# PSUM banks split 3/3/2, kernel rows by quarters, rows three blocks ahead, first loads in one queue, and dummy matmuls at the start

## The chip, the cores and the metric

The kernel runs on one core of a Trainium2 chip. The metric is the device time in microseconds of one execution. Lower is better.

## What is computed

The program computes a layer and all its gradients. The input x (2048 tokens, D = 576) is normalised, and three branches are added:

```python
xn  = layernorm(x)                                # over D
out = x + S4(xn) + FFN(xn)
# S4: y = irfft(rfft(xn) * rfft(K))[:L] + xn * Dskip, one kernel K of 2048 taps for each of 576 channels
dt  = exp(log_dt); logdA = dt * (A_re + 1j * A_im)
P   = exp(logdA[:, :, None] * l)                  # 576 x 128 x 2048
K   = einsum("dn,dnl,dn->dl", C, P, dt * B).real
# FFN: gate = xn @ W_gate; up = xn @ W_up        (576 x 4608)
#      h = gate * (gate > 0) * up; h @ W_down    (4608 x 576)
```

It returns `out` and the gradients of x, the six S4 parameter arrays, log_dt, Dskip and the three FFN weights for a given `grad_out`. Inputs and outputs are bf16.

## The kernel before

Two generators make the program, and a main loop interleaves them.

**FFN** (`Ffn.gen`). The hidden dimension is cut into 12 chunks of 384. In a chunk the tokens go by in four groups (`sg`) of four blocks of 128. `a_unit` multiplies one group by 128 columns of gate, up and down weights (L235, three PSUM tiles one after the other), and ACT and DVE make hT, dgT and duT from them (L243 to L255). `t_steps` turns these with PE (L264) for the weight gradients. `outdx` makes the output and the gradient of xn for one block of 128 tokens (L291: four PSUM groups of 3, 3, 6 and 6 matmuls of 288 columns), each group copied to `osx` (L67), and adds the tile to `acc_dram` by a DMA on POOL's queue (L304). After the last group of a chunk come the weight gradients: `dw_down` in four blocks (L329, 48 matmuls each), `dw_gu` in four (L345) and `dw_left` (L363). Each of these nine blocks needs one `rows` tile, which `rows` loads (L316) from the pool `ffn_d` of three buffers; block i asks for the blocks up to i + 2, and the first three of a chunk are asked for in its third group.

**S4** (`S4.gen`). The convolution is a transform in two steps with matrices of 128 and 16 points. It works in two halves of 288 channels. `p1` transforms xn and the gradient (`fwd1` L590, `mix` L604 and L605), multiplies them, and goes back to the kernel's gradient dk, which is kept whole in SBUF and stored with one DMA (L701). `p2` makes the kernel K and the sums for the parameter gradients, four channels at a time: DVE forms Y (L821 to L824), PE multiplies and turns it (`turn`, L849 and L859), `sums` multiplies it by dk (L873) and DVE reduces it (L877, L878); K goes to `k_dram` in groups of 32 channels (L852). `p3` loads K in one DMA (L710), transforms it and forms the S4 parts of the output and the gradient, stored to `C_ydu` (L742). The order is p1 of half 0; p2 of half 0 with p1 of half 1; p2 of half 1 with p3 of half 0; p3 of half 1.

**Order of the work.** Each step yields an estimate of its PE time, and S4 steps follow FFN steps in the ratio `PACE` = 0.9. S4 starts once all four layernorm groups are written. In the last chunk, `Final` adds the S4 parts to the FFN's, and all that is left of S4 is written before it. A DMA that waits on a queue (SP carries nearly all, POOL those of `acc_dram` and `xs_dram`, ACT those of `wf`) holds what comes after it on this queue. The order of instructions on an engine in the profile is not always that of the source: the load of x for the second group, for one, stands on SP ahead of the stores of the first.

**PSUM.** Eight banks are cut into three pools: `psum_mm` (FFN, 4 tiles), `psum_s4` (S4, 2 tiles) and `psum_t` (transposes for FFN and layernorm, 2 tiles). `Balance.copy` (L55 to L69) sends each copy out of PSUM to DVE or ACT by a running sum of estimated work, to which `bal.add` adds.

**The start.** `ln_group` loads x, makes mean and variance on DVE (L126, L127), normalises (L143, L144), turns the result (L147, L148) and stores it three times (`xT_dram`, `xn_dram`, and `xs_dram` on POOL's queue, L152). For the first group the down weights and the first block of `gT` are loaded in between, and `first` (L202) does the matmuls that need no layernorm while x is worked on.

Of the kernel before, what the change touches and what calls it, by code (L numbers as in the profile page):

```python
# [14 lines left out]
P = 128  # L15
# [6 lines left out]
ST = 16  # L22
# [12 lines left out]
PACE = 0.9  # L35
W1, W2, W3 = 60.0, 400.0, 58.0
# [41 lines left out]
def make_consts(g):  # L78
    nc, consts = g.nc, g.consts
    g.ident_bf = consts.tile([P, P], BF16, name="ident_bf")  # L80
    make_identity(nc, g.ident_bf[:])
    g.ident_f = consts.tile([P, P], F32, name="ident_f")
    make_identity(nc, g.ident_f[:])
    g.hpcol = consts.tile([P, 1], F32, name="hpcol")
    nc.vector.memset(g.hpcol[:], math.pi / 2)
    warm = consts.tile([P, 1], F32, name="warm")
    nc.scalar.activation(warm[:], g.hpcol[:], ACT.Sqrt)
    g.rinv = consts.tile([P, ST], F32, name="rinv")
    g.dsk_acc = consts.tile([P, NK, NSG], F32, name="dsk_acc")
# [15 lines left out]
def ln_group(g, pools, sg, loads=None, grad=None):  # L105

    nc, bal = g.nc, g.bal
    sb, small = pools
    t0 = sg * JS
    x4 = sb.tile([P, JS, D], BF16, name="x4")  # L110
    if sg == 0:
        for j in range(0, JS, 2):
            nc.sync.dma_start(x4[:, j:j + 2], g.x_v[:, j:j + 2, :])
        loads[0]()
    else:
        nc.sync.dma_start(x4[:], g.x_v[:, t0:t0 + JS, :])
    gT = g.xtp.tile([P, NK, JS * P], BF16, name="gT")
    nc.sync.dma_start(gT[:], g.gT_in[sg])
    if sg == 0:
        loads[1]()  # L120
        grad(gT)
    mv = small.tile([P, JS, nc.vector.BN_AGGR_DIM], F32, name="mv")
    for j in range(JS):
        stats = small.tile([P, 2, nc.vector.BN_STATS_DIM], F32, name="stats")
        for s in range(2):
            nc.vector.bn_stats(out=stats[:, s, :], in_=x4[:, j, s * DH:(s + 1) * DH])  # L126
        nc.vector.bn_aggr(out=mv[:, j, :], in_=stats[:])  # L127
    mvb = small.tile([P, JS, 2], BF16, name="mvb")
    nc.vector.tensor_copy(mvb[:], mv[:])
    mvf = small.tile([P, JS, 2], F32, name="mvf")  # L130
    nc.vector.tensor_copy(mvf[:], mvb[:])
    veb = small.tile([P, JS], BF16, name="veb")
    nc.vector.tensor_scalar(veb[:], mvf[:, :, 1], 1e-5, None, op0=ALU.add)
    sdb = small.tile([P, JS], BF16, name="sdb")
    nc.scalar.activation(sdb[:], veb[:], ACT.Sqrt)
    sdf = small.tile([P, JS], F32, name="sdf")
    nc.vector.tensor_copy(sdf[:], sdb[:])
    nc.vector.reciprocal(g.rinv[:, t0:t0 + JS], sdf[:])
    xn4 = sb.tile([P, JS, DP], BF16, name="xn4")
    nc.gpsimd.memset(xn4[:, :, D:DP], 0.0)  # L140
    xT = g.xtp.tile([P, NK, JS * P], BF16, name="xT")
    for j in range(JS):
        nc.vector.tensor_scalar(x4[:, j, :], x4[:, j, :], mvf[:, j, 0:1], None, op0=ALU.subtract)  # L143
        nc.vector.tensor_scalar(xn4[:, j, 0:D], x4[:, j, :], g.rinv[:, t0 + j:t0 + j + 1], None, op0=ALU.mult)  # L144
        pt = g.psum_t.tile([P, 8, P], BF16, name="pt")
        for k in range(NK):
            nc.tensor.transpose(out=pt[:, k, :], in_=xn4[:, j, k * P:(k + 1) * P], identity=g.ident_bf[:])  # L147
        nc.vector.tensor_copy(xT[:, :, j * P:(j + 1) * P], pt[:, 0:NK, :])  # L148
    nc.sync.dma_start(g.xT_dram[sg], xT[:])
    nc.sync.dma_start(g.xn_dram[:, t0:t0 + JS, :], xn4[:, :, 0:D])  # L150
    for k, d0, dsz in dchunks():
        nc.gpsimd.dma_start(g.xs_dram[k][:, t0:t0 + JS, :], xn4[:, :, d0:d0 + dsz])  # L152
    bal.add(d=7.5, a=0.3)
    return xT, gT

class Ffn:
    def __init__(self, g, ctx, Wd_in, Wf_in, dWg, dWu, dWd):
# [15 lines left out]
        self.dp = pool("ffn_d", 3)  # L173
# [10 lines left out]
    def load_wf(self, c):  # L184

        self.g.nc.scalar.dma_start(self.wf[:], self.Wf_in[c])

    def load_x(self, c, sg):
        g, nc = self.g, self.g.nc
        xT = g.xtp.tile([P, NK, JS * P], BF16, name="xT")  # L190
        nc.sync.dma_start(xT[:], g.xT_dram[sg])
        gT = g.xtp.tile([P, NK, JS * P], BF16, name="gT")
        nc.sync.dma_start(gT[:], g.gT_in[sg])
        self.X[(c, sg)] = (xT, gT)
# [112 lines left out]
    def rows(self, c, i):  # L307

        g, nc = self.g, self.g.nc
        for n in range(i, min(i + 3, 4 + NK)):  # L310
# [59 lines left out]
    def gen(self, ln, final):  # L370

        lu = FTC - 1
        for c in range(NFC):
            if c == 0:
                self.X[(0, 0)] = ln(0, (lambda: self.load_wd(0, (2,)), lambda: self.load_wd(0, (0, 1))), self.first)
                self.load_wf(0)
                for ft in range(FTC):
                    yield from self.a_unit(0, 0, ft)
                self.X[(0, 1)] = ln(1)
# [23 lines left out]
            for sg in range(1, NSG):  # L403
                todo = list(range(JS))
                for ft in range(FTC):
# [6 lines left out]
                    if c == 0 and ft == 0 and sg < 3:  # L412
                        self.X[(0, sg + 1)] = ln(sg + 1)
# [45 lines left out]
class S4:  # L459
    def __init__(self, g, par_in, log_dt, outs, Dskip):  # L460
# [8 lines left out]
        self.dk_dram = two("dk_dram", [P, DH // SC, ST, SC])  # L469
        self.k_dram = two("k_dram", [P, DH // SC, ST, SC])  # L470
# [108 lines left out]
    def fwd1(self, hf, ns, load, ap, n):  # L579
# [3 lines left out]
        for n2 in range(ST):  # L583
            if n2 % 2 == 0:
                S1, sig = Sx.get(n2 // 2), sigs.get(n2 // 2)
            A = ap.tile([P, ns, 2, DH], BF16, name=f"fA{ns}")
# [55 lines left out]
    def p1(self, hf, n, gap):  # L642
# [3 lines left out]
        with ExitStack() as c:  # L646
# [7 lines left out]
            yield from self.fwd1(hf, 2, load, ap, n)  # L654
# [29 lines left out]
        with ExitStack() as c:  # L684
            bp = self.pool(c, f"p1_c{hf}", n + 1, "right")
            dk = self.pool(c, f"p1_d{hf}", 1, "right").tile([P, DH // SC, ST, SC], BF16, name="dk")
# [6 lines left out]
            for n2 in range(ST):  # L693
# [5 lines left out]
                g.bal.copy(dk[:, :, n2, :], self.back2(S3[:, n2 % 2], Ct, 0).rearrange("p (g d) -> p g d", d=SC), DH)  # L699
                yield 0.5  # L700
            nc.sync.dma_start(self.dk_dram[hf][:], dk[:])  # L701

    def p3(self, hf, n, gap):

        g, nc, bal = self.g, self.g.nc, self.g.bal
        with ExitStack() as c:
            kp = self.pool(c, f"p3_k{hf}", 1, "right")
            ap = self.pool(c, f"p3_a{hf}", n, "right")
            kk = kp.tile([P, DH // SC, ST, SC], BF16, name="kk")
            nc.sync.dma_start(kk[:], self.k_dram[hf][:])  # L710
            yield gap
            yield from self.fwd1(hf, 1, lambda m: (lambda i, n2: kk[:, :, n2, :]), ap, n)
        with ExitStack() as c:
# [13 lines left out]
            for h in range(ST + 1):  # L727
# [9 lines left out]
                if old is not None:  # L737
                    Ct = fp.tile([P, 2, 2, DH], BF16, name="fC2")
                    for i in range(2):
                        yield from self.back1(Ct, i, old[i])  # L740
                        yield 0.7
                    nc.sync.dma_start(self.rows(self.C[2][hf], h - 1), Ct[:])  # L742
# [9 lines left out]
    def p2(self, hf, pools, pw):  # L752
# [12 lines left out]
        def load_dk(i):  # L765
            dkr = dkp.tile([P, ST, SC], BF16, name="dkr")
            nc.sync.dma_start(dkr[:], self.dk_dram[hf][:, i])
            return dkr
        exq, dkq = Ahead(load_ex, DH // SX, 2), Ahead(load_dk, DH // SC, 2)
        for gi in range(DH // SC):  # L770
# [7 lines left out]
            for x0 in range(0, SC, SX):  # L778
# [34 lines left out]
                for dd in range(x0, x0 + SX, DG):  # L813
# [5 lines left out]
                    U = uvp.tile([P, DG, 2, P], BF16, name="U")  # L819
                    V = uvp.tile([P, DG, 2, P], BF16, name="V")  # L820
                    v.tensor_tensor(vw(U), Ap(0), Bp(1), op=ALU.mult)  # L821
                    v.tensor_tensor(vw(V), Ap(1), Bp(0), op=ALU.mult)  # L822
                    Y = yop.tile([P, DG, 2, P], BF16, name="Y")
                    v.tensor_tensor(Y[:], U[:], V[:], op=ALU.add)  # L824
# [16 lines left out]
    def turn(self, item, ytp, turned):  # L841
# [9 lines left out]
        if dd + DG == SC:  # L851
            nc.sync.dma_start(self.k_dram[hf][:, gi], Kst[:])  # L852
# [193 lines left out]
def kernel(  # L1046
# [33 lines left out]
    g.psum_mm = pool("psum_mm", 4, space=PSUM)  # L1080
    g.psum_s4 = pool("psum_s4", 2, space=PSUM)
# [14 lines left out]
    ln_pools = [lnctx.enter_context(tc.tile_pool(name=n, bufs=4)) for n in ("ln_sb", "ln_small")]  # L1096
    done = [0]
# [83 lines left out]
```

## Time and profile before

| | us |
|---|---|
| median of 3 runs | 1874.34 |
| lowest and highest | 1871.84, 1876.11 |
| the profiled execution | 1874.97 |
| its span, first to last instruction | 1873.2 |

| engine | busy us | share of the span |
|---|---|---|
| PE (matmul) | 1759.1 | 94% |
| DVE | 1329.5 | 71% |
| ACT | 1161.1 | 62% |
| POOL | 216.9 | 12% |

The mean granted TensorE clock was 0.987, and the DMA queues moved 373.26 MB, 199 GB/s on average. A row of the page reads: line, engine, operation, output and inputs by name, shapes, count | busy time, mean ns of one | idle time of that engine just before, and what ended most of it. A row of waits reads: the waiting engine and line, what ended the wait, us in total, times, longest. A row of the timeline reads: start and length in us, engine, line, operation, count, and in brackets the idle time before it and its releaser. `ps_s_...` in the profile are the tiles of `psum_s4`, `ps_mm` those of `psum_mm`, `pt` those of `psum_t`. PE's row of a matmul includes the time in which it drains, which overlaps the next one.

### The profile page before, as it was taken

To read this page: it belongs to the slowest core of one execution; us is meant where nothing else is said; L and a number is where in the kernel's file an instruction comes from. 1 tells how busy PE (TensorE), PEld (TensorE's weight loads), DVE (VectorE), ACT (ScalarE), POOL (GpSimd) and SP (SyncE) were. 2 spreads that over 40 slices of the span, in tenths; PEclk is the share of its full clock that TensorE was granted. 3 is DMA by queue.
4 is the path that set the end of the run, shared out by engine and by line. 5 is a ranking of instruction groups with operands and counts; after the bars stand their busy time and mean duration, and the time that the engine had idled before them with its cause. 6 is when DMAs were issued, how large, how long until landed. Compare 5 with 4: busy or idle time off the path is not lost.

```text
span 1873.2 us, 41646 instructions
## 1 busy us (share of the span) xinstructions
PE 1759.1 (94%) x16246; PEld 1220.9 (65%) x16389; DVE 1329.5 (71%) x3052; ACT 1161.1 (62%) x2606; POOL 216.9 (12%) x264
## 2 busy tenths in 40 slices
PE   6988998999999999999899999999999998999989
PEld 3665556667667666766666766766766765676656
DVE  7574693678687787686597789787887863743872
ACT  3875775687487477477367658658747735742442
POOL 3200012022012002102101101102201100110000
PEclk9999999999999999999999999999999999999999
DMA  9698989567557566767756746855745759884763
GB/s 330 205 332 292 318 230 274 193 155 215 171 136 190 185 165 154 201 172 179 221 156 157 224 148 140 222 166 120 213 146 127 172 181 260 250 242 153 250 206 119
DMA packets 186106, 373.26 MB, mean 199 GB/s; under 512 B 19826, under 2 KB 95604, under 8 KB 183860
## 3 DMA queue, kind: packets, MB, share of 16 engines
q1 hardware_dynamic: 158900, 300.39, 48.1%
q0 software_dynamic: 25280, 54.28, 18.2%
q10 hardware_dynamic: 1728, 15.93, 2.4%
q8 instruction: 128, 2.10, 0.4%
q14 instruction: 70, 0.57, 0.1%
HBM read 233.08 MB, written 137.43 MB: 198 GB/s over the span
## 4 chain that ended last, share of the span: by engine, by line
PE 48%; DVE 16%; DMA 10%; ACT 8%; issue 6%; POOL 1%; SPq 1%; ACTq 0%; DVEq 0%; POOLq 0%
PE ps_mm L235 12%; PE ps_mm L291 10%; PE ps_mm L345 10%; PE ps_mm L329 4%; DMA acc_dram<-osx 3%; DMA rows<-in_gq_dram 3%; PE pt L264 2%; DVE pr L877 2%; DVE Sm L878 1%; DMA f_xg<-in_grad_out_dram 1%; PE ps_mm L363 1%; DVE Y L824 1%; DVE U L821 1%; ACT osx L67 1%; DVE V L822 1%
## 5 line engine op out<-in xcount | busy, mean ns | idle before, releaser
L67 ACT CAST osx<-ps_mm 128x288 bf16<-128x288 f32 x679 | 259.1, 426 | 73.2 <-PE ps_mm L291 56.9
L304 POOL DMA_DIRECT2D acc_dram<-osx x160 | 139.4, 875 | 1112.2 <-ACT osx L67 770.8
L291 PE MATMUL ps_mm<-wf,dgT 128*128 128x288 bf16 x1152 | 209.3, 286 | 2.2 <-ACT dhb L67 0.9
L291 PE MATMUL ps_mm<-wf,duT 128*128 128x288 bf16 x1152 | 208.2, 287 | 0.0
L345 PEld LDWEIGHTS <-rows 128*128 128x128 bf16 x1536 | 146.3, 98 | 91.0 <-issue 2.5
L291 PE MATMUL ps_mm<-wf,hT 128*128 128x288 bf16 x1152 | 186.7, 288 | 1.2 <-DVE hT L247 0.8
L235 PE MATMUL ps_mm<-xT,wd_97 128*128 128x512 bf16 x712 | 182.2, 380 | 0.5
L235 PE MATMUL ps_mm<-gT,wd_98 128*128 128x512 bf16 x697 | 180.9, 384 | 0.3
L329 PE MATMUL ps_mm<-rows,hN 128*128 128x144 bf16 x2304 | 163.7, 231 | 16.8 <-DMA rows<-in_gq_dram 15.2
L235 PE MATMUL ps_mm<-xT,wd_96 128*128 128x512 bf16 x593 | 168.6, 380 | 7.0 <-DVE xT L148 0.6
L329 PEld LDWEIGHTS <-hN 128*128 128x128 bf16 x2304 | 152.8, 100 | 20.0 <-DMA rows<-in_gq_dram 9.3
L245 DVE SCALAR_TENSOR_TENSOR upm<-rg,ps_mm 128x512 bf16<-128x512 bf16 x144 | 98.4, 683 | 92.4 <-PE ps_mm L235 66.5
L345 PE MATMUL ps_mm<-dgN,rows 128*128 128x384 bf16 x768 | 140.2, 328 | 0.0
L345 PE MATMUL ps_mm<-duN,rows 128*128 128x384 bf16 x768 | 138.4, 326 | 0.0
L67 ACT CAST obw<-ps_mm 128x384 bf16<-128x384 f32 x106 | 50.5, 477 | 140.0 <-PE ps_mm L345 101.6
L291 PEld LDWEIGHTS <-duT 128*128 128x128 bf16 x1152 | 112.5, 98 | 32.7 <-issue 4.1
L291 PEld LDWEIGHTS <-dgT 128*128 128x128 bf16 x1152 | 109.5, 98 | 31.7 <-issue 5.7
L291 PEld LDWEIGHTS <-hT 128*128 128x128 bf16 x1152 | 107.8, 98 | 29.1 <-DVE hT L247 3.0
L824 DVE TENSOR_TENSOR Y<-U,V 128x1024 bf16<-128x1024 bf16 x144 | 99.0, 687 | 38.2 <-PE ps_s_4388 L859 20.9
L243 ACT ACTIVATE rg<-ps_mm 128x512 bf16<-128x512 f32 x144 | 87.0, 604 | 61.8 <-PE ps_mm L235 57.5
L67 ACT CAST dhb<-ps_mm 128x512 bf16<-128x512 f32 x141 | 83.8, 594 | 63.8 <-PE ps_mm L235 61.4
L878 DVE TENSOR_REDUCE Sm<-pr 128x8 f32<-128x256 f32 x288 | 119.9, 416 | 4.6
(2893 smaller groups left out, 3567.5 us busy)
## 6 DMA issues: line engine op xcount, KB each, us to landing
acc_dram<-osx POOLq DMA_DIRECT2D x176, 288.0 KB, 4.8
gT<-in_gT_dram SPq DMA_DIRECT2D x48, 640.0 KB, 5.8
xT<-xT_dram SPq DMA_DIRECT2D x44, 640.0 KB, 5.2
rows<-in_gq_dram SPq DMA_DIRECT2D x48, 576.0 KB, 4.9
wf<-in_Wf_dram ACTq DMA_DIRECT2D x12, 1296.0 KB, 8.7
ex_dram<-exs SPq DMA_DIRECT2D x18, 640.0 KB, 4.5
ex<-ex_dram SPq DMA_DIRECT2D x36, 320.0 KB, 3.5
out_dram<-obw SPq DMA_DIRECT2D x96, 96.0 KB, 2.4
```

The lines of the kernel that those rows point to most:

```text
L67: self.nc.scalar.copy(out, in_)
L235: nc.tensor.matmul(ps[:], lhsT=w[:, k, fs], rhs=rhs[:, k, :], start=(k == 0), stop=(k == NK - 1))
L243: nc.scalar.activation(rg[:], ps_g[:], ACT.Relu)
L245: nc.vector.scalar_tensor_tensor(upm[:], rg[:], 0.0, ps_u[:], op0=ALU.is_gt, op1=ALU.mult)
L264: nc.tensor.transpose(out=pt[:, j, :], in_=src[:, j * P:(j + 1) * P], identity=g.ident_bf[:])
L291: nc.tensor.matmul(ps[:, :DH], lhsT=lt, rhs=rh, start=(i == 0), stop=(i == len(mms) - 1))
L304: nc.gpsimd.dma_start(g.acc_dram[:, t, :, :], o[:], accum_op=ALU.add)
L329: nc.tensor.matmul(ps[:, ft * 144:(ft + 1) * 144], lhsT=self.hN[:, st, ft * P:(ft + 1) * P], rhs=gq[:, st, :], start=(st == 0), stop=(st = ...
L345: nc.tensor.matmul(ps[:, :Fc], lhsT=xs[:, st, 0:P], rhs=src[:, st, :], start=(st == 0), stop=(st == ST - 1))
L824: v.tensor_tensor(Y[:], U[:], V[:], op=ALU.add)
L877: nc.vector.tensor_tensor(pr[:], X[:, dx:dx + DG, r0:r0 + 2].rearrange("p d r a -> p d (r a)").unsqueeze(2).to_broadcast(sh), psg[:, 0:DG ...
L878: nc.vector.tensor_reduce(out=Sm[:, vi, s0 + dd:s0 + dd + DG, :], in_=pr[:], op=ALU.add, axis=AX.X)
```

## The change

The pools get 3, 3 and 2 banks. `ffn_d` gets a fourth buffer, and `rows` asks for blocks up to i + 3. dk is stored, and K loaded, in four pieces of four rows each, through two rotating tiles; both DRAM tensors are laid out by quarters, so that the loads of dk by 32 channels, and the stores of K, are made of runs of 256 bytes. `fwd1` takes the `gap` yield of its caller and gives it after its first loads are issued; `p1` had none there. `C_ydu` is stored in two halves. The first product of Y is written to Y itself, and U is gone.

At the start all x groups, the weights and `wf` are loaded on SP's queue in a fixed order; `wf` is no longer on ACT's for the first chunk. 60 matmuls of 128 columns on the identity, into a `psum_s4` tile that nothing uses but one small copy, precede all others. Half of the subtractions and of the xT copies of the layernorm go to ACT, and the `xs_dram` stores from POOL's queue to SP's.

```diff
+WARM = 60
...
+    ps = g.psum_s4.tile([P, 512], F32, name="ps_s4")
+    for i in range(WARM):
+        nc.tensor.matmul(ps[:, 0:P], lhsT=g.ident_bf[:], rhs=g.ident_bf[:], start=True, stop=True)
+    nc.scalar.copy(warm[:], ps[:, 0:1])
...
+def ln_load(g, sb, sg, pieces=1):
+    nc = g.nc
+    x4 = sb.tile([P, JS, D], BF16, name="x4")
+    n = JS // pieces
+    for j in range(0, JS, n):
+        nc.sync.dma_start(x4[:, j:j + n], g.x_v[:, sg * JS + j:sg * JS + j + n, :])
+    return x4
...
-        nc.vector.tensor_scalar(x4[:, j, :], x4[:, j, :], mvf[:, j, 0:1], None, op0=ALU.subtract)
+        if j % 2 == 0:
+            nc.vector.tensor_scalar(x4[:, j, :], x4[:, j, :], neg[:, j:j + 1], None, op0=ALU.add)
+        else:
+            nc.scalar.activation(x4[:, j, :], x4[:, j, :], ACT.Identity, bias=neg[:, j:j + 1])
+    for j in range(JS):
...
-        nc.vector.tensor_copy(xT[:, :, j * P:(j + 1) * P], pt[:, 0:NK, :])
+        (nc.vector.tensor_copy if j % 2 == 0 else nc.scalar.copy)(xT[:, :, j * P:(j + 1) * P], pt[:, 0:NK, :])
...
-        nc.gpsimd.dma_start(g.xs_dram[k][:, t0:t0 + JS, :], xn4[:, :, d0:d0 + dsz])
-    bal.add(d=7.5, a=0.3)
+        nc.sync.dma_start(g.xs_dram[k][:, t0:t0 + JS, :], xn4[:, :, d0:d0 + dsz])
+    bal.add(d=6.5, a=2.5)
...
-        self.dp = pool("ffn_d", 3)
+        self.dp = pool("ffn_d", 4)
...
-        for n in range(i, min(i + 3, 4 + NK)):
+        for n in range(i, min(i + 4, 4 + NK)):
...
-                self.X[(0, 0)] = ln(0, (lambda: self.load_wd(0, (2,)), lambda: self.load_wd(0, (0, 1))), self.first)
-                self.load_wf(0)
+                xs = [ln_load(g, self.ln_sb, 0, 2)]
+                self.load_wd(0, (2,))
+                gT = self.load_gT(0)
+                self.load_wd(0, (0, 1))
+                xs.append(ln_load(g, self.ln_sb, 1))
+                self.load_wf(0, g.nc.sync)
+                xs += [ln_load(g, self.ln_sb, sg) for sg in (2, 3)]
+                self.first(gT)
+                self.X[(0, 0)] = ln(0, xs[0], gT)
...
-        self.dk_dram = two("dk_dram", [P, DH // SC, ST, SC])
-        self.k_dram = two("k_dram", [P, DH // SC, ST, SC])
+        self.dk_dram = two("dk_dram", [P, 4, DH // SC, 4, SC])
+        self.k_dram = two("k_dram", [P, 4, DH // SC, 4, SC])
...
                 S1, sig = Sx.get(n2 // 2), sigs.get(n2 // 2)
+                if n2 == 0:
+                    yield gap
...
-            dk = self.pool(c, f"p1_d{hf}", 1, "right").tile([P, DH // SC, ST, SC], BF16, name="dk")
+            dp = self.pool(c, f"p1_d{hf}", 2, "right")
...
+                if n2 % 4 == 0:
+                    dk = dp.tile([P, DH // SC, 4, SC], BF16, name="dk")
...
+                if n2 % 4 == 3:
+                    nc.sync.dma_start(self.dk_dram[hf][:, n2 // 4], dk[:])
...
+            def load(m):
+                if m % 2 == 0:
+                    kks[0] = kp.tile([P, DH // SC, 4, SC], BF16, name="kk")
+                    nc.sync.dma_start(kks[0][:], self.k_dram[hf][:, m // 2])
+                kk = kks[0]
+                return lambda i, n2: kk[:, :, n2 % 4, :]
+            yield from self.fwd1(hf, 1, load, ap, n, gap)
...
-                    Ct = fp.tile([P, 2, 2, DH], BF16, name="fC2")
                     for i in range(2):
-                        yield from self.back1(Ct, i, old[i])
+                        Ct = fp.tile([P, 1, 2, DH], BF16, name="fC2")
+                        yield from self.back1(Ct, 0, old[i])
+                        nc.sync.dma_start(self.rows(self.C[2][hf], h - 1)[:, i:i + 1], Ct[:])
...
-                    v.tensor_tensor(vw(U), Ap(0), Bp(1), op=ALU.mult)
+                    v.tensor_tensor(vw(Y), Ap(0), Bp(1), op=ALU.mult)
                     v.tensor_tensor(vw(V), Ap(1), Bp(0), op=ALU.mult)
-                    v.tensor_tensor(Y[:], U[:], V[:], op=ALU.add)
+                    v.tensor_tensor(Y[:], Y[:], V[:], op=ALU.add)
...
-            nc.sync.dma_start(self.k_dram[hf][:, gi], Kst[:])
+            nc.sync.dma_start(self.k_dram[hf][:, :, gi], Kst[:].rearrange("p (q a) d -> p q a d", q=4))
...
-    g.psum_mm = pool("psum_mm", 4, space=PSUM)
-    g.psum_s4 = pool("psum_s4", 2, space=PSUM)
+    g.psum_mm = pool("psum_mm", 3, space=PSUM)
+    g.psum_s4 = pool("psum_s4", 3, space=PSUM)
```

## The prediction

> **What bounds the kernel now.** I read the busy shares and slices of the page first, then the waits of PE, then the timeline at the three places where PE's slices are below 9.
>
> ```profile
> PE 1759.1 (94%) x16246; PEld 1220.9 (65%) x16389; DVE 1329.5 (71%) x3052; ACT 1161.1 (62%) x2606; POOL 216.9 (12%) x264
> PE   6988998999999999999899999999999998999989
> PEclk9999999999999999999999999999999999999999
> ```
>
> PE is the bound: no other engine is above 71%. A matmul that stops no one costs its slot (the chain of waits has twelve L291 matmuls in 1.47 us, 0.1225 us each, although the row says 286 ns, because their ends overlap), so only what lengthens the row of slots can be won or lost. PE is idle for 1873.2 - 1759.1 = 114.1 us. The waits of PE say for what:
>
> ```profile
> PE ps_mm L329 <- DMA rows<-in_gq_dram: 15.2, 6, 5.1
> PE ps_mm L202 <- DMA gT<-in_gT_dram: 11.0, 1, 11.0
> PE ps_s_25857 L590 <- ACT fA_25837 L67: 3.1, 1, 3.1
> PE ps_s_4243 L590 <- DMA sig<-xn_dram: 3.0, 1, 3.0
> PE ps_s_17634 L859 <- DVE pr L877: 1.9, 1, 1.9
> PE ps_mm L329 <- ACT osx L67: 1.5, 2, 1.0
> ```
>
> Added up, all rows of this view: the start 11.0; rows 15.2; matmuls into ps_s4 behind ACT or DVE 37.0, in some sixty small rows; matmuls into ps_s4 behind a DMA 10.5; transposes for FFN and layernorm 16.2; matmuls into ps_mm behind ACT or DVE 6.2. The small pool of two banks waits, the large one of four hardly does. A further cost stands in no row of waits: the mean granted clock is 0.987, so about 0.013 x 1873 = 24 us of clock are lost, in stretches that follow an idle PE:
>
> ```profile
> 20.00:34.00 14.00, 10.72 (x60) 5.48 (x61) 13.75 (x46) 2.85 (x6) 3.60 (x5) 0.88 1.04 373
> 296.00:312.00 16.00, 10.76 (x85) 8.29 (x85) 0.00 (x0) 5.76 (x16) 8.34 (x8) 0.79 1.02 287
> 905.00:925.00 20.00, 15.02 (x149) 12.62 (x146) 14.71 (x33) 2.74 (x5) 2.52 (x2) 0.83 0.72 232
> ```
>
> (Columns: stretch, length, then busy time of PE, PEld, DVE, ACT, POOL, the clock, the DMA share, GB/s.)
>
> **The start.**
>
> ```profile
> 11.02 5.87 PE L202 MATMUL ps_mm<-gT,wd_98 128*128 128x512 bf16 x15 [11.02 <-DMA gT<-in_gT_dram]
> 19.17 1.24 PE L235 MATMUL ps_mm<-xT,wd_96 128*128 128x512 bf16 x5 [0.58 <-DVE xT L148]
> 29.88 1.25 PE L147 MATMUL pt<-ident_bf,xn_350 128*128 128x128 bf16 x10 [0.86 <-DVE xn_350 L144]
> 31.72 1.93 PE L235 MATMUL ps_mm<-xT,wd_96 128*128 128x512 bf16 x5
> ```
>
> wf (1.3 MB) now leaves on ACT's queue at 0.82 us and shares the DMA engines with x, wd2 and gT (1.7 MB). The change queues it behind x1. At the 311 to 361 GB/s of these microseconds, 1.7 MB land about 5 us after the first 2 us, so gT is there near 7 us, not at 11.0. The fifteen L202 matmuls take 0.427 us each, against 0.216 us for the L235 ones from 19.17 on: they run at half rate, 15 x 0.21 = 3.2 us. The sixty dummies address that. The Trainium skill (TensorE: Matmul & The Clock Gate, The HAM clock gate) says that the array starts at half clock, needs about 3.4 us of sustained work to be released, and falls back after a comparable idle time. By that rule the dummies, waiting only for the identity (1.5 us), run 32 at 107 ns and 28 at 56 ns (the page's gaps, so an estimate) and end near 6.6 us; with gT at 7 us the release holds and 3.2 us are won, with gT at 11 us it is lost again and they win nothing. The trace alone (clock 0.5 from about 30 us, after PE's waits for xn_350) says the same about falling back; I take the win. Should the clock stay at half, 60 x 107 ns ends at 8 us and delays first by 1 us. x lands about 2.5 us earlier too, so the first L235 comes at about 13.5, not 19.2. In 20 to 34 us DVE is the bound (13.75 of 14 us). Each layernorm group loses two subtractions (0.34 us each), two xT copies (0.49) and one cast (0.17) to ACT or nothing, about 1.8 of 10 us, and pays one neg (0.17). PE's full flow at 31.7 should begin near 26. Against it: ACT, at 17.1 of 20 us in 60 to 80, gets this work; SP takes over 20 xs stores (POOL 0.76 us each; SP's DMA issues take 0.33 to 0.6, so 10 us of SP time), which wait there for xn with gT of the next group behind them, needed only by a third matmul group 10 us later. I take -6 us; bounds +2 and -11.
>
> **Rows ahead.** Only the fourth block of a chunk is late: three buffers hold blocks 0 to 2 some 95 us early, while block 3 is asked for when block 0 has been used (L316 at 610.2, 908.5, 1671.1), and needs 6 to 9 us to land, against two blocks of 48 matmuls at 0.0625 us, 6 us, plus whatever S4 puts between. At 908 it is worse because SP stands at the kk load:
>
> ```profile
> 899.99 0.33 SPq L852 DMA_DIRECT2D k_dram_135<-Kst  x1
> 908.04 0.33 SPq L710 DMA_DIRECT2D kk<-k_dram_135  x1
> 908.46 0.38 SPq L316 DMA_DIRECT2D rows<-in_gq_dram  x1
> ```
>
> With four buffers block 3 is early like the others, and each later block one block earlier. The 15.2 us go, and the half clock after 142, 914 and 1680 us (1.7 + 3.4 + 1.7 us by the clock of those stretches). The copies and stores that caught up meanwhile, and the next late transfer, take some back: -17; bounds -6 and -22. SP still waits at kk for the last Kst store; behind it only later rows and dkr then stand, with a block to spare.
>
> **Quarters and gaps.** At the first hand-over SP waits until 291.9 for one 1152 KB dk store (7.4 us to landing) before dkr, and the sig loads leave at 294.4: PE waits 3.0 us at 299.1 and runs at half clock until 309 (3.4 us lost). The last quarter store is a fourth of the size, and fwd1 now yields its gap (3 us of FFN work) after the loads are issued. -4; bounds +1 and -8. The added gaps (10 and 3 us) put S4's end about 14 us later in FFN's time; S4 ends at 1665.6 and its outputs are first needed at 1723, so 57 us of cover hide it. If that cover were gone, its last steps would run alone, at most those 14 us.
>
> Costs: C_ydu in halves, 32 more stores of 0.33 us on SP; dk and kk quarters, 6 more each; together 15 us of SP time over the span, hidden while SP is not late. Each half store waits for its own evictions, with b_k and s_ug loads behind it; the waits of SP at L723 are 61.7 us now and hardly reach PE (3.7 us, once). dkr loads and Kst stores now have runs of 256 bytes, 36 x 512 = 18432 packets. No such packet is in the trace; the nearest, 512 or 576 bytes, took 31 ns each, which makes 0.57 ms over 16 engines, 36 us of DMA time in a stage of 1200 us at a share of 0.61 to 0.76. The Trainium skill's page DMA: Bandwidth & Descriptors (Specifications) says that below 512 bytes a transfer no longer runs at line rate, which speaks against this edit: twice the price, an estimate, would be 72 us, 6% of the stage, and dkr is asked for a whole group ahead. I take +3 for all this; bounds 0 and +12. Y in place of U costs DVE nothing (the same three products); it only moves the wait for a Y buffer from L824 two instructions up, with its 20.9 us (once, near 293 to 314) unchanged.
>
> **PSUM 3/3/2.** What two banks cost S4:
>
> ```profile
> 315.98 0.36 PE L873 MATMUL ps_s_4489<-dkc,YT 128*128 128x32 bf16 x8
> 316.38 0.42 DVE L877 TENSOR_TENSOR pr<-X,ps_s_4489 128x256 f32<-128x256 f32 x1 [0.28 <-PE ps_s_4489 L873]
> 316.44 0.35 PE L849 MATMUL ps_s_4520<-XC,Y 128*128 128x16 bf16 x8
> 316.83 0.21 ACT L67 CAST Kst<-ps_s_4520 128x64 bf16<-128x64 f32 x1 [0.44 <-PE ps_s_4520 L849]
> 317.09 0.61 PE L859 MATMUL ps_s_4530<-ident_bf,Y 128*128 128x128 bf16 x8
> 317.29 0.42 DVE L877 TENSOR_TENSOR pr<-X,ps_s_4489 128x256 f32<-128x256 f32 x1
> ```
>
> The sums' bank is read twice by DVE and held to 317.7; so the transposes of L859 wait for the Kst copy of the other bank and start 50 ns after it. With a third bank they need not. The 37.0 us of the view are too small, since a matmul's drawn end hides the first 0.16 us of every wait; from start to start against the slots I count about 75 us at ps_s4. Of these some 18 stay (single waits where ACT itself was held up, as at 155, 306, 1002 and 1570, and the stretch 90 to 115 where ACT is busy 22.6 of 25 us). Of the other 57 I take 60%, -34: PE arrives earlier, the evictions do not. Bounds -57 and -10.
>
> The price is at ps_mm. I set each ps_mm group's first matmul beside the end of the eviction three groups before it, from the same timeline: 98 of about 1350 groups would start before it, by 40 us in total, 25 us when a delay already suffered is not counted again. They are outdx groups (slots of 0.37 us, an eviction of 0.43 us on ACT, often behind a 0.6 us hN copy), and groups after an a_unit, which takes all three banks while the up bank waits for DVE. I take +20; bounds +2 and +40.
>
> Sum: -6 - 17 - 4 + 3 - 34 + 20 = -38 us. The profiled execution took 1874.97, of which 1.8 us lie around its span, 0.6 above the median of 1874.34: 1836.
>
> **Rivals.**
> - The stalls only change pool. PE's lead is bounded by the six banks together, and these stay six; S4's 34 come back at ps_mm. For it: ACT does 679 of 704 osx copies. Against it: 37.0 beside 6.2 us is no balanced split. Then -24: 1850.
> - Slower: three banks serve FFN as badly as two serve S4. Place: a_unit followed by outdx in 1100 to 1500, where DVE is busy about 80 of each 100 us and upm frees the up bank late. S4 pays 35 ns (view) to 72 ns (slots) for each of 1046 allocations; FFN has about 1350, so 47 to 97 us. It decides from +58 at ps_mm (43 ns each). At 75 us: 1874 + 17 = 1891.
> - More: every removed stop also keeps the clock full (half of the 24 us), and S4's waits vanish nearly whole: -60, 1814.
> - The dummies find gT late, or the rows are late by another transfer: the start and rows give 10, not 23: 1849, inside the first rival's place.
>
> **How the numbers follow.** The forecast 0.47, stalls change pool (with late gT) 0.27, more 0.13, slower 0.10, nothing measurable 0.03. A measurement of this kernel can tell about 0.2%, 3.7 us, from no change. Faster: 0.47 + 0.13 + 0.26 = 0.86; same 0.04; slower 0.10. The range runs from 1804, past the "more" case, to 1868, past the changed pool; outside it lie the slower case and nothing measurable.
>
> **What would show it.** Right: L202 near 7.5 us at 0.216 us a matmul; no PE row L329 <- DMA rows; ps_s4 rows under 15 us; ps_mm rows behind ACT or DVE between 10 and 30; clock above 0.99. Wrong: ps_mm rows above 50 us; L235 and L291 waiting for upm and osx through 1100 to 1500; rows still late; S4 alone at the end.

## The result and the profile after

The changed kernel took 1860.6 us (median of four runs, 1856.6 to 1864.5) beside 1875.1 us for the kernel before: a ratio of 0.9926, 95% interval 0.9901 to 0.9950. That is 14 us faster; 38 were forecast. Two later sets of runs gave 0.9934 and 0.9930, so 12 to 14 us is a firm number. The profiled execution took 1864.5 us with a span of 1862.4, and its mean granted clock was 0.991 instead of 0.987.

The engines' busy time and PE's slices, from the page after:

```profile
PE 1753.3 (94%) x16449; PEld 1222.3 (66%) x16449; DVE 1327.2 (71%) x3041; ACT 1164.1 (63%) x2618; POOL 204.7 (11%) x244
PE   7989999999999999999989999999999998989889
```

PE is still the bound, with 109 us of idle time instead of 114. Its largest waits after the change (waiting engine and line, what ended the wait, us in total, times, longest):

```profile
PE ps_mm L300 <- ACT osx L68: 9.8, 21, 2.2
PE ps_mm L211 <- DMA gT<-in_gT_dram: 8.7, 1, 8.7
PE pt L273 <- DVE dgT L262: 6.5, 4, 2.6
...
PE ps_s_25937 L608 <- ACT fA_25907 L68: 4.7, 1, 4.7
...
PE ps_s_4087 L657 <- DMA bC_4031<-C_dk_191: 3.7, 1, 3.7
PE ps_s_27457 L622 <- ACT fC_27423 L70: 3.5, 1, 3.5
```

No row of PE waiting for `rows` is left. What is new is the first row, FFN's outdx (L300, L291 before) waiting for its eviction; before, it was 0.2 us. The last two rows are longer than any of their kind before, where the longest wait for bC was 1.4 us and the longest for fC 1.1. All rows of this view summed, for the kernels that this document turns on (us; a wait at ps_mm that a DMA ended is in a column of its own; the clock is that of the profiled execution):

| | ps_s behind ACT, DVE | ps_mm behind ACT, DVE | ps_mm behind a DMA | mean clock |
|---|---|---|---|---|
| before | 37.0 | 6.2 | 26.2 | 0.987 |
| before with 3/3/2 alone (e5) | 14.3 | 32.1 | 25.0 | 0.993 |
| changed | 36.0 | 34.7 | 8.7 | 0.991 |
| changed with 4/2/2 (e1) | 57.1 | 11.9 | 10.1 | 0.992 |
| best version (e11) | 20.1 | 31.2 | 15.0 | 0.991 |

The second and third lines hold the case. The third bank brings S4's waits in this view from 37 to 14 when it comes alone. In the whole change they are back at 36: other parts of the change put new ones in their place.

### The profile page after: what moved, and what is told of

Its sections match the earlier page's. It is cut to its first block, busy times and chain, and to the rows that moved or that the text cites. A ratio compares the mean times of both kernels' runs of the same rounds, so it can differ in the third digit from the quotient of the medians.

```text
span 1862.4 us, 42002 instructions
## 1 busy us (share of the span) xinstructions
PE 1753.3 (94%) x16449; PEld 1222.3 (66%) x16449; DVE 1327.2 (71%) x3041; ACT 1164.1 (63%) x2618; POOL 204.7 (11%) x244
## 4 chain that ended last, share of the span: by engine, by line
PE 52%; DVE 22%; DMA 12%; ACT 8%; issue 5%; SPq 1%; POOL 1%; ACTq 0%; DVEq 0%; POOLq 0%
PE ps_mm L244 13%; PE ps_mm L300 12%; PE ps_mm L354 10%; PE ps_mm L338 6%; DMA acc_dram<-osx 3%; PE pt L273 2%; DVE pr L902 2%; DVE Sm L903 2%; DVE Y L849 2%; DMA f_xg<-in_grad_out_dram 2%; DVE V L848 1%; DVE Y L847 1%; DVE upm L254 1%; DMA ex_dram<-exs 1%; PE ps_mm L372 1%
## 5 line engine op out<-in xcount | busy, mean ns | idle before, releaser
L300 PE MATMUL ps_mm<-wf,dgT 128*128 128x288 bf16 x1152 | 205.6, 287 | 16.6 <-ACT osx L68 9.8
L300 PE MATMUL ps_mm<-wf,duT 128*128 128x288 bf16 x1152 | 206.1, 287 | 0.0
L300 PE MATMUL ps_mm<-wf,hT 128*128 128x288 bf16 x1152 | 184.3, 288 | 6.0 <-DVE hT L256 3.5
L244 PE MATMUL ps_mm<-xT,wd_158 128*128 128x512 bf16 x720 | 180.1, 379 | 4.0 <-DVE osx L62 1.9
L244 PE MATMUL ps_mm<-xT,wd_159 128*128 128x512 bf16 x720 | 180.0, 379 | 0.0
L338 PE MATMUL ps_mm<-rows,hN 128*128 128x144 bf16 x2304 | 161.1, 228 | 0.0
L338 PEld LDWEIGHTS <-hN 128*128 128x128 bf16 x2304 | 150.7, 99 | 7.4 <-issue 4.1
L300 PEld LDWEIGHTS <-dgT 128*128 128x128 bf16 x1152 | 110.2, 98 | 54.0 <-issue 27.5
L354 PE MATMUL ps_mm<-dgN,rows 128*128 128x384 bf16 x768 | 136.4, 326 | 0.6 <-ACT rg L252 0.6
L300 PEld LDWEIGHTS <-duT 128*128 128x128 bf16 x1152 | 112.7, 98 | 29.1 <-issue 0.5
L300 PEld LDWEIGHTS <-hT 128*128 128x128 bf16 x1152 | 108.0, 98 | 34.3 <-DVE hT L256 5.4
L244 PEld LDWEIGHTS <-wd_160 128*128 128x128 bf16 x705 | 64.7, 98 | 67.9 <-issue 12.9
```

Source lines behind the costliest of these rows:

```text
L244: nc.tensor.matmul(ps[:], lhsT=w[:, k, fs], rhs=rhs[:, k, :], start=(k == 0), stop=(k == NK - 1))
L300: nc.tensor.matmul(ps[:, :DH], lhsT=lt, rhs=rh, start=(i == 0), stop=(i == len(mms) - 1))
L338: nc.tensor.matmul(ps[:, ft * 144:(ft + 1) * 144], lhsT=self.hN[:, st, ft * P:(ft + 1) * P], rhs=gq[:, st, :], start=(st == 0), stop=(st = ...
L354: nc.tensor.matmul(ps[:, :Fc], lhsT=xs[:, st, 0:P], rhs=src[:, st, :], start=(st == 0), stop=(st == ST - 1))
```

## The experiments

The kernel before ran beside each set of runs (1871.1 to 1873.8 us). Ratios are against it, with 95% intervals. Microseconds in the text are the differences of ratios times 1873. Within 0.2%, about 4 us, two single ratios can't be told apart.

### Which bank split is it?

The changed kernel with the old split (e1), the changed kernel again (e4), and the kernel before with nothing but the new split (e5).

```diff
 e1: from the changed kernel
-    g.psum_mm = pool("psum_mm", 3, space=PSUM)
-    g.psum_s4 = pool("psum_s4", 3, space=PSUM)
+    g.psum_mm = pool("psum_mm", 4, space=PSUM)
+    g.psum_s4 = pool("psum_s4", 2, space=PSUM)
 e5: from the kernel before, the same lines the other way round
```

> The changed kernel with the PSUM pools back at 4, 2 and 2; all else of the change stays. Theory A (the split won nothing, because what S4 gained at its third bank came back at ps_mm): within 4 us of the changed kernel's 1860.6, with PE's ps_mm rows behind ACT or DVE falling from 34.7 to about 6 us and its ps_s4 rows rising from 36 to 45 or more. Rival B (the forecast's: the split is worth about 14 us): 1872 to 1877. Rival C (the split itself lost time): 1850 to 1856.

> The changed kernel itself, as the level for the others on this chip: 1857 to 1864, 0.9926 of the kernel before.

> The kernel before with only the PSUM pools at 3, 3 and 2. Theory A (the split is a gain of its own, as the 10.7 us between the changed kernel with and without it say): 1861 to 1866, PE's ps_s4 rows behind ACT or DVE down from 37 to 15 to 22 us, its ps_mm rows up from 6 to about 25 us. Rival B (the split pays only together with the rest, because the delayed S4 needs the bank): within 3 us of 1873.8. Forecast on record: -14 (1860).

Measured: e1 1872.6 us (0.9988, 0.9975 to 1.0001), e4 1861.9 (0.9934, 0.9910 to 0.9958), e5 1860.5 (0.9931, 0.9910 to 0.9951). The split is worth 13 us alone and 10 us within the change. Waits of PE in e5 (its line numbers are those of before):

```profile
PE ps_mm L291 <- ACT osx L67: 14.5, 22, 2.1
PE ps_mm L329 <- DMA rows<-in_gq_dram: 13.8, 6, 4.0
...
PE ps_s L590 <- ACT fA L67: 5.9, 10, 1.7
```

The first row is the price at ps_mm, where the prediction put it: outdx behind the osx copy on ACT. The second shows that the late `rows` were left untouched. e5 alone is as fast as the whole change; the other parts of it together brought nothing.

PE's idle time in e5 is what it was (113.6 us, 114.1 before); the gain lies in PE's busy time, 1741.5 us instead of 1759.1 for as many matmuls. Busy time takes in the short waits, since a matmul's drawn end covers the first 0.16 us of the next one's wait. Counted from start to start, as the prediction counted (each matmul's start less the start of the one before, less the slot of the earlier one's shape at full clock), the traces give for matmuls behind ACT or DVE:

| us | ps_s | ps_mm |
|---|---|---|
| before | 75 | 11 |
| e5 | 30 | 49 |
| e1 | 99 | 17 |
| changed | 53 | 52 |

The split takes 45 us from S4's waits and puts 38 on FFN's when it comes alone, 46 and 35 within the change. The view of waits shows no gain because S4's were many and short: 283 starts late by over 12 ns at ps_s before, 121 in e5. (The profiled execution of e5 is the fastest of its six, 18 us below that of before, so these shares are rough.)

### Rows ahead

The changed kernel with `rows` asked for two blocks ahead and three buffers.

```diff
-        self.dp = pool("ffn_d", 4)
+        self.dp = pool("ffn_d", 3)
...
-        for n in range(i, min(i + 4, 4 + NK)):
+        for n in range(i, min(i + 3, 4 + NK)):
```

> The changed kernel with rows only two blocks ahead and three buffers, as before. Theory A (the fourth buffer wins the 15 us of waits at block 3 and 4 to 7 us of clock): 1876 to 1884, with PE's L338 rows behind a rows DMA back at 12 to 20 us. Rival B (S4, two steps further on, is late in place of the rows, and half of it comes back): 1868 to 1873, with as many waits on rows.

Measured: 1879.4 us (1.0027, 1.0011 to 1.0044), 17 us slower than the changed kernel. The row of the wait is 9 us of it:

```profile
PE ps_mm L338 <- DMA rows<-in_gq_dram: 9.3, 7, 5.6
```

The mean granted clock over e8's twelve runs was 0.987, over the six of the changed kernel beside e1 (e4) 0.991; 0.004 of 1870 us is an estimated 8 us, about the rest. So the fourth buffer is worth what was forecast, 17 us, by late rows and the half clock behind them. With 13 for the banks it makes 30, and 14 were seen: if the parts add up, others must cost some 16 us.

### The start

The changed kernel with the dummies on a zero tile that DVE sets first (e3), and the kernel before with the new start but no dummies (e6).

```diff
 e3: from the changed kernel
+    zero = consts.tile([P, P], BF16, name="zero")
+    nc.vector.memset(zero[:], 0.0)
...
-        nc.tensor.matmul(ps[:, 0:P], lhsT=g.ident_bf[:], rhs=g.ident_bf[:], start=True, stop=True)
+        nc.tensor.matmul(ps[:, 0:P], lhsT=zero[:], rhs=zero[:], start=True, stop=True)
 e6: from the kernel before: ln_load, the loads of gen, ln_group, load_wf and first as in the change
```

> The changed kernel, with the sixty dummy matmuls on a tile of zeros that DVE sets first, so that they stand first on PE instead of behind the first L211 matmul. Theory A (in the changed kernel they lie between gT's landing and the fourteen other L211 matmuls, 4.8 us of PE on the path): L211 runs from about 8.7 to 12 us at 0.216 us each, the first matmuls of the layernorm group come 4 to 5 us earlier, and the whole is 3 to 5 us shorter, 1856 to 1858. Rival B (DVE's layernorm of the second group bounds the start anyway): L211 done by 12 but PE's steady flow still from 28.6, the whole within 1.5 us of 1860.6. Rival C (the clock falls back before gT lands): L211 at 0.427 us each.

> The kernel before with only the start of the change (loads in SP's one queue, half of the subtractions and xT copies on ACT, xs stores on SP), without the dummies. Theory A (the start wins its 5 to 6 us, seen as 6 us at the first weight gradients, and keeps them): 1867 to 1870. Rival B (what is won at the start is waited away when S4 and its loads come, since DVE, ACT and the DMAs are busy from 73 us on): 1872 to 1875.

Measured: e3 1862.2 us (0.9938, 0.9921 to 0.9956), e6 1876.0 (1.0006, 0.9994 to 1.0019). Neither the new start nor the right place for the dummies moves the time. The timeline of PE after (start and length in us, then the idle time and its releaser in brackets):

```profile
8.74 0.58 PE L211 MATMUL ps_mm<-gT,wd_160 128*128 128x512 bf16 x1 [8.74 <-DMA gT<-in_gT_dram]
9.12 4.80 PE L91 MATMUL ps_s_83<-ident_bf 128*128 128x128 bf16 x60
13.75 3.19 PE L211 MATMUL ps_mm<-gT,wd_160 128*128 128x512 bf16 x14
...
28.57 1.24 PE L244 MATMUL ps_mm<-xT,wd_158 128*128 128x512 bf16 x5 [0.52 <-ACT xT L153]
```

gT lands 2.3 us earlier than before. But on PE's queue one matmul of `first` (L211) stands ahead of the sixty dummies, so all of them wait for gT. They do release the clock: the fourteen others come 0.216 us apart. Before, twelve of the fifteen L202 matmuls came 0.427 us apart and the last three 0.216. The dummies' own 4.8 us take that back, and PE goes on from `first` at 16.8 us, against 16.7 before. Full flow starts at 28.6, not 31.7.

In e3 they run while gT is on its way:

```profile
1.07 6.16 PE L93 MATMUL ps_s<-zero 128*128 128x128 bf16 x60 [1.07 <-DVE hpcol L88]
8.52 3.40 PE L213 MATMUL ps_mm<-gT,wd 128*128 128x512 bf16 x15 [1.29 <-DMA gT<-in_gT_dram]
...
23.47 2.55 PE L154 MATMUL pt<-ident_bf,xn 128*128 128x128 bf16 x20 [2.36 <-DVE xn L151]
```

`first` ends near 11.8, five microseconds earlier, and at 23.5 PE has stood 2.4 us for DVE's xn. In 20 to 34 us of e3 the granted clock is down to 0.76 (1.00 in the changed kernel):

```profile
20.00:34.00 14.00, 10.65 (x67) 6.07 (x65) 11.50 (x43) 7.54 (x15) 0.00 (x0) 0.76 0.90 244
```

The lead is gone at once: the first outdx comes at 33.8 us in e3 and at 32.9 in the changed kernel. PE waited for the second layernorm group on DVE, and half clock followed the wait. In e6 the gain of the start is there at first, and fades: against before, the first outdx comes 3.7 us earlier (33.1 and 36.8), the first weight gradients 2.9 us (125.9 and 128.7), the end not at all. Where the 2.9 us go is not shown.

### Quarters of dk and K

The kernel before with dk stored and K loaded in quarters, the two layouts and the runs of 256 bytes, and p3's gap moved behind its loads; p1 gets no gap.

```diff
-        self.dk_dram = two("dk_dram", [P, DH // SC, ST, SC])
-        self.k_dram = two("k_dram", [P, DH // SC, ST, SC])
+        self.dk_dram = two("dk_dram", [P, 4, DH // SC, 4, SC])
+        self.k_dram = two("k_dram", [P, 4, DH // SC, 4, SC])
...
+                if n2 % 4 == 3:
+                    nc.sync.dma_start(self.dk_dram[hf][:, n2 // 4], dk[:])
...
+                    nc.sync.dma_start(kks[0][:], self.k_dram[hf][:, m // 2])
```

> The kernel before with only dk and K moved by quarters: four stores of dk, four loads of K, runs of 256 bytes in the small loads and stores; no gap is added to p1, and rows stay two ahead. Forecast on record: hand-over -4, 256-byte runs and DMAs +3. Theory A (that sum is about right): 1871 to 1875. Rival B (the runs of 256 bytes and the further stores cost S4 more, which is where the missing 10 us went): 1879 to 1884, with the dkr loads and Kst stores landing several us later.

Measured: 1878.2 us (1.0015, 0.9999 to 1.0032), so 0 to 6 us slower. At the first hand-over the prediction expected the sig wait to shrink. The wait of PE in 280 to 330 us, and the stretch, in e7, then the first sig matmul before and in e7:

```profile
PE ps_s L592 <- DMA sig<-xn_dram: 3.0, 1, 3.0
```

```profile
296.00:312.00 16.00, 14.51 (x176) 12.08 (x175) 4.22 (x8) 8.68 (x23) 2.13 (x3) 0.89 1.05 301
```

```profile
299.07 0.28 PE L590 MATMUL ps_s_4243<-sig,Sx 128*128 128x288 bf16 x1 [3.04 <-DMA sig<-xn_dram]
295.10 0.28 PE L592 MATMUL ps_s<-sig,Sx 128*128 128x288 bf16 x1 [3.02 <-DMA sig<-xn_dram]
```

The wait is as long as before (3.0 us), but 4 us earlier. The last store of dk is issued at 281.3 and holds SP until 286.8, 5.5 us instead of 7.4 (284.5 to 291.9), and the sig loads leave at 290.2 instead of 294.4. PE, too, comes 4 us earlier to this matmul (292.1 and 296.0), so it stands as long as before. Which of the parts of e7 makes it slower (more stores, the runs of 256 bytes, the moved gap) is not shown.

### Half stores of C_ydu

In the changed kernel each half of `fC2` is a tile of its own, in the pool where the whole one had two buffers. A half comes back after one step of p3 instead of two, so the next copy waits until the store of the half before last has landed. Timeline of ACT and PE after:

```profile
1649.96 0.41 ACT L70 ACTIVATE fC_27329<-ps_s_27334 128x288 bf16<-128x288 f32 x1
1657.81 0.41 ACT L70 ACTIVATE fC_27423<-ps_s_27424 128x288 bf16<-128x288 f32 x1 [4.25 <-DMA C_ydu_194<-fC_27329]
1658.27 0.40 PE L622 MATMUL ps_s_27457<-b_k,CC 128*128 128x288 bf16 x1 [3.53 <-ACT fC_27423 L70]
```

The copy of tile 27329 was done at 1650.4, its store landed near 1657.8, ACT stood 4.25 us for the buffer and PE 3.53 us for ACT. ACT's waits of this kind add up to 20 us after the change, and there is none before. In e2 the halves get a pool of their own, with two buffers in half 0 and four in half 1. In e11 it has three and four, and p1's gap is gone as well (next section).

```diff
 e2: from the changed kernel
+            fq = self.pool(c, f"p3_q{hf}", 2 + 2 * hf, "right")
...
-                        Ct = fp.tile([P, 1, 2, DH], BF16, name="fC2")
+                        Ct = fq.tile([P, 1, 2, DH], BF16, name="fC2")
 e11: 3 + hf buffers, and the gap in p1 is 0.0
```

> The changed kernel, with the half tiles fC2 in a pool of their own that has four buffers in p3 of half 1 (two in half 0, as now); the stores stay in halves. Theory A (a half tile comes back after one step of p3 instead of two, so ACT waits for the C_ydu store to land, 20 us of ACT's idle time between 1586 and 1674): ACT's waits for C_ydu vanish in that stage, p3 of half 1 ends 8 to 10 us earlier, the whole 1850 to 1854. Rival B (the stage is longer because S4 starts it later and because of more DMAs, not because of the buffers): 1858 to 1862, and C_ydu stays as late.

> The changed kernel, with the halves of C_ydu in a pool of their own of three buffers in half 0 and four in half 1 (two shared ones in the changed kernel; two and four gave 1855.6), and without the gap in p1. If half 0 suffers from the two buffers as half 1 did (2 us of waits for fC in 1160 to 1400): 1852 to 1854; with the gap as the cost as well, 1846; if neither matters, 1855.6.

Measured: e2 1855.6 us (0.9904, 0.9886 to 0.9921), 6 us faster than the changed kernel (0 to 11 by the two intervals), with 6.9 us of ACT's waits for the store left (two, at 1641 and 1647 us, the last twenty microseconds of S4). PE's waits at ps_s behind ACT and DVE fell from 36.4 (e4) to 27.5. e11: 1848.8 us (0.9866, 0.9848 to 0.9884); ACT has no wait for C_ydu left.

### The gap in p1

The changed kernel with p1's gap taken away (e9, and e15 again in another set, beside e16, the changed kernel).

```diff
-            yield from self.fwd1(hf, 2, load, ap, n, gap)
+            yield from self.fwd1(hf, 2, load, ap, n, 0.0)
```

> The changed kernel, but the first transform of p1 gets a gap of 0 again. The changed kernel took 1861.9; the parts measured one by one (banks -13, rows -17.5, start +1, quarters +3, half stores of C_ydu +6) add to -20, and -12 was measured, so about 7 us are unassigned. If the added gap, which puts S4 some 14 us later against FFN, is what costs them: about 1855. If it only shifts the order, with as much work left at the end: 1860 to 1864.

> The changed kernel without the gap in p1 once more, beside the two others: 1852 to 1855, as at first.

> The changed kernel once more, beside the three others: 1860 to 1863.

Measured: e9 1853.5 us (0.9888, 0.9871 to 0.9904), e15 1856.0 (0.9908, 0.9889 to 0.9927), e16 1860.5 (0.9930, 0.9910 to 0.9950). Against e4 the gap costs 9 us, within the second set 4.

After e9 I had an explanation. In before, S4's last matmul starts at 1665.6 us, two microseconds ahead of chunk 10's weight gradients (first L329 at 1667.9). In the changed kernel it starts at 1671.5, 24 us into them (first L338 at 1647.9), and that stage takes 58 us instead of 45 with e9. If the place of S4's end were the price, it could be moved alone: e13 keeps p1's gap and takes p3's away; e14 has none in p1 and a longer one in p3.

```diff
 e13: from the changed kernel
-            yield from self.p3(1, 4, 8.0)
+            yield from self.p3(1, 4, 0.0)
 e14: from e9
-            yield from self.p3(1, 4, 8.0)
+            yield from self.p3(1, 4, 20.0)
```

> The changed kernel with its gaps in p1, but the two gaps of p3 in half 1 are 0 instead of 8, so that S4 ends some 16 us earlier against FFN. If the price of the gap in p1 is where S4 ends (24 us behind the start of chunk 10's weight gradients, 3 us ahead of it without the gap): 1853 to 1857. If it is paid where the gap stands, early in the program: 1861 to 1863. If the loads of p3 are late without their gaps: above 1864.

> The changed kernel without the gap in p1 (1853.5), but the two gaps of p3 in half 1 are 20 instead of 8, so that S4 ends some 24 us later against FFN, as far in chunk 10's weight gradients as in the changed kernel. If the end's place is the price: 1860 to 1863. If the gap in p1 is paid early: 1852 to 1855.

Measured: e13 1861.3 us (0.9937, 0.9919 to 0.9955), e14 1853.5 (0.9895, 0.9876 to 0.9914). Starts of matmuls in us, from each trace:

| | p1's gap | chunk 10's weight gradients, first | S4's last matmul | chunk 10's weight gradients, last | chunk 11's, first | span |
|---|---|---|---|---|---|---|
| changed (e16) | yes | 1649.3 | 1673.0 | 1707.5 | 1822.3 | 1862.4 |
| e13 | yes | 1659.2 | 1652.1 | 1704.2 | 1821.5 | 1861.6 |
| no gap (e15) | no | 1649.9 | 1647.6 | 1695.0 | 1813.6 | 1853.7 |
| e14 | no | 1634.4 | 1672.3 | 1693.2 | 1812.8 | 1853.2 |

The explanation fell. The end moved by 21 and 25 us as meant, and the stage went from 58 to 45 us (e13) and from 45 to 59 (e14), but the stretch before it changed by nearly as much the other way: only S4's slots had moved. The pairs with one setting of p1's gap end within 1 us of each other. Three contrasts of the gap (9, 4, and 8 us from e13 to e14) average 7 us.

Where it is paid can be bounded from PE's waits. In 100 to 560 us the gap saves: 19.4 us of waits in e16 beside 28.3 in e15. From 560 to 1700 it loses: 53.1 beside 34.1. The ends of FFN's chunks say it more closely. With S4 put off, FFN is ahead: when chunk 3 ends, by 16, 13 and 13 us in the three pairs (e16 and e15, e4 and e9, e13 and e14); when chunk 6 ends, by 6, 3 and 2. So some 10 us are lost in chunks 4 to 6 (counted from 0), each time. These chunks in e16 and then in e15:

```profile
641.80:1090.00 448.20, 428.12 (x4239) 302.08 (x4270) 341.12 (x736) 294.87 (x664) 60.24 (x62) 0.99 0.67 178
658.00:1095.90 437.90, 422.92 (x4210) 298.14 (x4242) 337.91 (x736) 293.43 (x658) 57.04 (x60) 1.00 0.68 181
```

In the three runs with the gap the clock is down to 0.50 for 3.4 us near 882 and again near 968 (the profile shown at the top has the second alone); in the three without, never in these chunks. At half speed that is an estimated 3.4 us of the 10. One of the rows that differ, in 560 to 900 us, is outdx behind its eviction, in e16 and then in e15:

```profile
PE ps_mm L300 <- ACT osx L68: 5.1, 7, 3.1
```

```profile
PE ps_mm L300 <- ACT osx L68: 2.9, 7, 1.4
```

No single wait carries the rest. The gap sets which S4 step stands beside which FFN step for the remaining run. That it is this alignment that costs the time is argued, not shown.

### Y in place of U, and the best version

The kernel before with Y in place of U alone (e10), and the kernel before with all parts of the change but the new start and p1's gap, with e11's buffers for the halves (e12).

```diff
 e10: from the kernel before
-                    U = uvp.tile([P, DG, 2, P], BF16, name="U")
+                    Y = yop.tile([P, DG, 2, P], BF16, name="Y")
...
-                    v.tensor_tensor(vw(U), Ap(0), Bp(1), op=ALU.mult)
+                    v.tensor_tensor(vw(Y), Ap(0), Bp(1), op=ALU.mult)
...
-                    v.tensor_tensor(Y[:], U[:], V[:], op=ALU.add)
+                    v.tensor_tensor(Y[:], Y[:], V[:], op=ALU.add)
```

> The kernel before, and only the product of Y written to Y itself, with U gone. The prediction took this for nothing: 1872 to 1876. If the unassigned 7 us sit here, because DVE's first product now waits for a Y buffer that PE still reads: 1878 to 1882.

> All parts but the start and the gap in p1: the kernel before with banks 3/3/2, rows three blocks ahead, dk and K in quarters, Y in place of U, halves of C_ydu with three and four buffers. Against the run beside it with the same parts and the new start it tells what the start is worth in the whole. If the start is worth nothing, as alone (+1): the same within 2 us. If the start's 3 to 6 us at the first chunk are kept: 3 to 6 us slower. If layernorm work on ACT and xs stores on SP cost more than they bring: 3 to 7 us faster.

Measured: e10 1876.4 us (1.0013, 1.0002 to 1.0024), 2 us slower, at the edge of what can be seen. e12 1851.7 us (0.9876, 0.9856 to 0.9896), beside 0.9866 for e11: the start is worth 2 us at most, and the intervals overlap. e11, with 1848.8 us, is the fastest kernel here, 25 us below before and 12 below the change.

## Why the prediction was wrong

The direction and the place of the two large gains (banks and rows) were right; the sum was not, because terms that it set at nothing, at a gain or too small were costs. Four of them make 24 of the 27 us between the two sums below: the start (7), the quarters (7), p1's gap (7) and the halves of C_ydu (3). By the prediction's own steps:

| step | forecast | measured | from |
|---|---|---|---|
| PSUM 3/3/2, net of -34 and +20 | -14 | -13 alone, -10 in the whole | e5, e1 |
| rows ahead | -17 | -17 | e8 to e4 |
| the start | -6 | +1 alone; 0 to -2 in the whole | e6, e12 to e11 |
| quarters and the moved gap | -4 | +3, runs of 256 bytes included (0 to 6) | e7 |
| p1's gap, "57 us of cover hide it" | 0 | +7 | e9, e13 to e16 |
| halves of C_ydu, runs of 256 bytes and further DMAs | +3 for all | +6 for the halves alone | e2 |
| Y in place of U | 0 | +2 | e10 |
| sum | -38 | about -11; -12 to -14 seen | |

(The last sum takes the first figures: -13 - 17 + 1 + 3 + 7 + 6 + 2.)

- **PSUM.** The net was right, its two terms were not: S4 got back 45 us and not 34, and FFN paid 38 and not 20, near the upper bound of 40. That leaves 7 us. The other 6 go with the clock, which this step left out: its mean over all runs was 0.9868 before and 0.9902 in e5, an estimated 6 us of 1870. So that -14 was met is in part luck; two misses and a missing term cancelled. Of the signs, "ps_s4 rows under 15 us" held in e5 (14.3) and failed in the whole change (36.0), where the price of the other steps stands in them; "ps_mm rows between 10 and 30" failed in both (32.1 and 34.7).
- **The rows** went as worked out in size; the wait is 9 us in e8 where 15 were read before, the half clock about as much as forecast (6.8).
- **The start.** Three steps failed. "Fifteen L202 matmuls at 0.427" was read from the first ones: the starts in the trace before double their rate at 16.1 us, so twelve ran slow and 2.5 us were to be had, not 3.2. The dummies were to end "near 6.6 us", waiting only for the identity, with gT "near 7 us" (it came at 8.7); in the program's order on PE they stand behind the first matmul that waits for gT, which the trace after shows and the source does not. And a gain in the first 35 us was taken over to the end, while the text itself had DVE as the bound of 20 to 34 us. e3 puts the dummies where the text had them and wins nothing; e6 wins 3.7 us by the first outdx and has none left at the end. So the last step is the one that counts.
- **The hand-over.** The 3.0 us at sig were put down to the store of dk ahead of it. With a store of a fourth (e7) sig does land 4 us earlier, but PE is there 4 us earlier as well and waits the same 3.0; the step took PE's arrival as fixed. In the whole change sig is no longer waited for, but PE waits up to 3.7 us for bC (L657), where 1.4 was the longest before. With p1's gap taken away (e9) 1.5 us of the sig wait are back.
- **The gap.** The reasoning looked only at when S4's outputs are needed. e13 and e14 confirm that half: S4's end can be moved over 20 us for nothing. The 7 us are paid on the way, most of it in chunks 4 to 6, and the prediction had no term for that.
- **The halves.** The prediction saw that "each half store waits for its own evictions" and looked at what stands behind it on SP. It did not ask when the buffer comes back. Two buffers of half the size give half the time for the store to land.

Of the rivals, "the stalls only change pool" is right on most of the waits, and not on the result: 38 of S4's 45 us came back at ps_mm, and the kernel is 13 us faster all the same. "Slower" would have needed 58 us at ps_mm; 38 were seen. Of the late-gT rival the first half came true, by the order on PE and not by a late load.

## What to carry to other kernels

When a tile is cut in half, count its buffers in time, not in number: how long from the end of the store's source copy until the same buffer is written again, against how long the store takes to land. Banks that two streams share are worth balancing by the waits of both, counted from start to start: a view that leaves out the first 0.16 us of each showed no gain in the sum (43 and 46 us) where 7 us were won. A yield, a gap or a store moved in an interleaved program shifts all that follows; price it by a run without it, since cover at its end says nothing about the new neighbours on the way.

## What was not expected of the hardware

- The granted clock of the windows shows 1.00 from 8 to 14 us, while matmuls of 128 columns start 0.107 us apart until 11.8 and 0.056 apart after it: at the start, the half rate is seen only in the matmuls' own spacing.
- How long PE ran before the rate doubled differs, by the starts of its matmuls: 3.1 us in the changed kernel (8.7 to 11.8), 3.6 and 4.5 in its profiles as e4 and e16, 3.7 in e6 (9.0 to 12.7), 5.1 in the kernel before (11.0 to 16.1) and 5.5 in e3 (1.1 to 6.6). The Trainium skill's page TensorE: Matmul & The Clock Gate (The HAM clock gate) gives about 3.4 us, and 0.5 us of variation because the activity window runs freely. That fits 3.1 to 3.7; the three longer ones lie outside.
- A store of a half tile of `fC2` (147 KB) took 7.4 us from its issue at 1650.4 to the release of its buffer at 1657.8, in a stretch with a DMA share of 0.95.
- Moving the xs stores from POOL's queue to SP's cut them into smaller packets: e6 has 30,066 packets under 512 bytes beside 19,826 before, and the 10,240 more are as many as 20 stores of 512 rows make. With e6 at 1.0006 of before they cost nothing that can be seen.
